# K in the outer loop of one product, and a V load placed behind two transposes, in a chunked attention and GELU kernel

## The chip, the cores and the metric

The kernel runs on one core of a Trainium2 chip. The metric is the device time of one execution in microseconds (us). The kernel before has a median of 274.94 us over three runs (272.26 to 277.09). Engines are named as the profile names them: PE is TensorE (PEld its weight loads), DVE VectorE, ACT ScalarE, POOL GpSimd, SP the engine that issues most of the transfers (SPq is its queue).

## The reference

Attention within chunks of 64 tokens, for 8 batches, 8 heads, 576 tokens and a head size of 64, and behind it a two-layer network with an exact GELU on the 4608 tokens (8 x 576) of width 512, with an inner width of 2048:

```python
scores = np.matmul(q_c, k_c.transpose(0, 1, 2, 4, 3)) / np.sqrt(D)
scores = scores - np.max(scores, axis=-1, keepdims=True)
attn = np.exp(scores)
attn = attn / (np.sum(attn, axis=-1, keepdims=True) + 1e-09)
x = np.matmul(attn, v_c)              # to (4608, 512): tokens by heads * head size
h = x @ w_in                          # (512, 2048)
g = 0.5 * h * (1.0 + erf(h / np.sqrt(2.0)))
out = g @ w_out                       # (2048, 512)
```

Inputs and output are float32; the products run in bfloat16 with float32 sums.

## The kernel before, in words

The tokens go in nine tiles of 512, numbered 0 to 8. Tiles 0 to 7 hold the first eight chunks of one batch each; tile 8 holds the ninth chunk of every batch, and its q, k and v are gathered by eight small loads each, one per batch. A tile goes through attention (which makes x, transposed, 512 by 512), mm1 (x times w_in and GELU, which makes h) and mm2 (h times w_out, which makes y). The main loop runs over t; its pass t does mm1 and mm2 of tile t and, in between the products of mm2, attention of later tiles. We call the pass "stage t".

The order of the work on every engine is the order in which the program is written: nothing reorders it later. Work that is to stand between products is handed over as lists of small functions: `e1` for mm1 (keyed by a word of a hand-written order such as `FOUR`) and `e2` for mm2 (keyed by a number from 0 to 5, called by `also(i)`).

From stage 3 on, mm2 is done with seven products of half size in place of eight (`mm2_seven`, for stages 3 to 7; stage 8 has its own, `last_seven`). h and w_out are cut into two by two blocks, and sums of blocks are multiplied. One such product has 16 matmuls of 128x128 weights by 128x256: two row blocks of 128 tokens (m), each summed over eight blocks of K (f), both halves in one PSUM bank. Its sums of h come from VectorE: s1 and s2 in pieces, at the words `h1`, `h2`, `h3` of mm1's order (blocks 0-1, 2-5 and 6-7; L549 and L550), s3 at L554 and s4 at L558. The order on TensorE in mm2 of stages 3 to 7 is:

- first product: h and w_out, into bank X, which ScalarE copies to bank Y (L752)
- at 1: attention times V of tile t + 1 (`rows_av`, L324). VectorE divides the result (L342, L344) into rows, and SP issues two transposes of these rows to x (`rows_x`, L336): one behind the second of six banks, one behind the sixth. Also at 1: casts and loads of q
- second product: s2 and T2, a difference of blocks of w_out, onto bank Y. This is the one that the change touches
- third product (onto X) and fourth (s1, onto Y)
- at 2: the scores of tile t + 2 (`quad_S`, L228), from q and k that SP transposed (`flip`, L189) during mm1
- fifth product (s3, bank Z), sixth (s4, onto Y), then at 4: four differences of blocks of x (`x_sums`, L595), which mm1 of the next stage needs from its fourth product on; then the seventh product (onto Z)

Stores of y (L815) stand behind the third, fifth, sixth and seventh products, on SP. SP also issues all loads (L102 to L141), in the order of the program. V of a tile comes in two halves (even heads, then odd heads: `load_v_rows(t, (0,))` and `(1,)`), into one arrival buffer of a pool of five; GpSimd casts both halves (L206) before `rows_av` reads them. For tile 8 the two halves are eight loads each: the first half is issued at the start of mm1 of stage 6, behind the transposes of q and k of tile 8 (`flips_of`), the second half and both casts at the start of stage 7.

Of the kernel before, what the change touches and what calls it, by code (L numbers as in the profile page):

```python
# [11 lines left out]
def kernel(  # L12
# [9 lines left out]
    nc = tc.nc  # L22
    P = 128
# [4 lines left out]
    B, H, S, D = q.shape  # L28
# [38 lines left out]
    FH, TH, NH = FF // 2, MT // 2, d_model // 2  # L67
# [17 lines left out]
    def stage_tile(pool=None):  # L85
        if pool is wsum:
            return wsum.tile([P, SW], f32, tag="wsum", name="arrival")
        return stage.tile([P, SW], f32, tag="stage", name="arrival")
# [26 lines left out]
    def load_v_rows(t, parity=range(2)):  # L115

        if "vf" not in tiles[t]:
            tiles[t]["vf"] = stage_tile()[:].rearrange("p (h n d) -> p h n d", h=H, d=D)
        raw = tiles[t]["vf"]

        def go(to, rows):
            nc.sync.dma_start(to, rows.rearrange("h key d -> key h d"))  # L122
        last = CT // 2 - 1
        if t < B and 0 in parity:
            for n in range(CT // 2):
                go(raw[:, 0::2, n], v[t, 0::2, P * n:P * (n + 1), :])
        if t < B and 1 in parity:
            for n in range(last):
                go(raw[:, 1::2, n], v[t, 1::2, CH + P * n:CH + P * (n + 1), :])
            go(raw[0:CH, 1::2, last], v[t, 1::2, MT - CH:MT, :])  # L130
            go(raw[CH:P, 1::2, last], v[t, 1::2, 0:CH, :])
        if t == B:
            for b in range(B):
                for r in parity:
                    c, n = place(r, b)
                    go(raw[CH * c:CH * (c + 1), r::2, n], v[b, r::2, MT:S, :])
# [13 lines left out]
    def place(r, i):  # L150

        return (i % 2, i // 2) if r == 0 else ((i + 1) % 2, (i - 1) % CT // 2)
# [47 lines left out]
    def cast_v_rows(t, copy):  # L200
        st = tiles[t]
        st["v"] = ld.tile([P, H, CT // 2, D + 1], bf16, tag="v", name="v_nat")
        if t >= FIRSTX:
            nc.gpsimd.memset(st["v"][:, :, :, D:], 1.0)
        for r in range(2):
            copy(st["v"][:, r::2, :, :D], st["vf"][:, r::2])  # L206
# [511 lines left out]
    def product(out, lhs, rhs, fresh, behind=lambda m: None):  # L718

        for m in range(TH // P):  # L720
            for f in range(FH):
                nc.tensor.matmul(out[m], lhs[:, f, m * P:(m + 1) * P], rhs[:, f, :],  # L722
                                 start=fresh and f == 0 and (m == 0 or len(out) == 3), stop=(f == FH - 1),
                                 skip_group_check=True)
            behind(m)

    def halves(bank):
        return [bank[:, 0], bank[:, 1]]

    def mm2_seven(t, at={}):  # L730

        def also(i):
            for u in at.get(i, ()):
                u()
        st = tiles[t]
        h = st["h"][:].rearrange("p (k f) (m e) -> p k f m e", k=2, m=2)
        w = w_out_sb[:].rearrange("p (k f) (n e) -> p k f n e", k=2, n=2)
        s = [None] + [st["s", i][:] for i in range(1, 5)]
        T = [None] + [w_t[i] for i in range(1, 5)]
        def bank_mm():  # L740
            return ps_mm.tile([P, 2, NH], f32, tag="mm", name="y_ps")
        X, Y = bank_mm(), bank_mm()
        s2, s5 = (work.tile([P, 2, NH], f32, tag=nm, name=nm, bufs=1) for nm in ("y_2", "y_5"))
        y = [ypool.tile([P, 2, d_model], f32, tag="y", name="y_sb") for _ in range(2)]
        TT, add = nc.vector.tensor_tensor, mybir.AluOpType.add
        if t == B:
            s1 = work.tile([P, 2, NH], f32, tag="y_1", name="y_1", bufs=1)
            last_seven(t, h, w, s, T, (X, Y, bank_mm()), (s1, s2, s5), y)
            return
        also(0)  # L750
        product(halves(X), h[:, 0, :, 0], w[:, 0, :, 0], True)
        AC(Y[:], X[:])  # L752
        Z = bank_mm()
        st["Z"] = Z[:].rearrange("p m n -> p (m n)")
        also(1)
        h_third(t)
        product(halves(Y), s[2], T[2], False)
        AC(s2[:], Y[:])
        product(halves(X), h[:, 1, :, 0], w[:, 1, :, 0], False)
        AC(y[0][:, :, :NH], X[:])  # L760
        store(t, 0, 0, y)
        product(halves(Y), s[1], T[1], False)
        AC(s5[:], Y[:])
        h_fourth(t)
        also(2)
        product(halves(Z), s[3], T[3], True)
        TT(y[1][:, :, NH:], Z[:], s5[:], op=add)
        store(t, 1, 1, y)
        also(3)
        product(halves(Y), s[4], w[:, 1, :, 1], False)  # L770
        AC(y[0][:, :, NH:], Y[:])
        store(t, 0, 1, y)
        also(4)
        product(halves(Z), h[:, 1, :, 1], T[4], False)
        TT(y[1][:, :, :NH], Z[:], s2[:], op=add)
        store(t, 1, 0, y)
        also(5)
# [144 lines left out]
    with tc.manual_schedule():  # L922
# [7 lines left out]
        T = att_units(0, DV, AC)  # L930
# [74 lines left out]
        T = att_units(1, AC, AC)  # L1005
# [15 lines left out]
        def flips_of(n):  # L1021
            for nm in "qk":
                flip(n, nm)
# [22 lines left out]
        for t in range(1, NT):  # L1046
            e1, e2 = {}, {}
            n = t + 1
            if n < NT:
                tiles[n]["x"] = xpool.tile([P, G, MT], bf16, tag="x", name="x")  # L1050
            if t == 1:
                flips_of(2)
                load_v_rows(2, (1,))
                cast_v_rows(2, PO)
                loads_of_qk(3)
                pool_cast_qk(3)
                e1 = {"1a": [lambda: w_in_sums(slice(0, 2), "c")], "p": [lambda: load_v_rows(3)], "end": [lambda: w_sums((1, 3))]}
                e2 = one_tile(2, {5: [lambda: act_table(Act.Gelu)],
                                  8: [lambda: flips_of(3), lambda: loads_of_qk(4)]})
            elif t == 2:  # L1060
                cast_v_rows(3, PO)
                pool_cast_qk(4)
                e1 = {f"i{g}": [lambda g=g: in_order(3, g)] for g in range(G)}
                e1.update({f"w{i}": [lambda i=i: w_sums((i,))] for i in (2, 4)})
                flips_of(4)
                load_v_rows(4)
                load_qk(5, "q")
                cast_v_rows(4, PO)
                e2 = one_tile(3, {8: [lambda: load_qk(5, "k")], 14: [lambda: quad_S(4)]})
            elif n < NT:  # L1070
                def ahead(t=t):
                    if FIRST7 < t < B - 2:
                        load_v_rows(t + 2)
                    if t + 2 < NT:
                        flips_of(t + 2)
                    if t == FIRST7:
                        load_ahead(t, "q")
                    if t == B - 2:
                        load_v_rows(B, (0,))
                    if t == B - 1:  # L1080
                        load_v_rows(B, (1,))
                        cast_v_rows(B, PO)

                def late_v(t=t):
                    load_v_rows(t + 2)
                    cast_v_rows(t + 2, PO)

                def behind(t=t):
                    load_ahead(t, "k")
                e1 = {"begin": [ahead]}  # L1090
                if t + 2 < NT:
                    e1["begin"] = [lambda t=t: pool_cast_k(t + 2), ahead]
                if t == FIRST7:
                    pool_cast_q(t + 2)
                    e1["tab"] = [lambda: act_table(Act.Gelu)]
                e2 = {1: [lambda: rows_av(n, tiles[n - 1]["Z"]), lambda: rows_x(n)], 2: [], 3: [], 4: [behind, lambda: x_sums(n)]}
                if t == FIRST7:
                    e2[2] += [late_v, lambda: w_in_sums(slice(0, 2), "d")]
                if FIRST7 < t < B - 2:
                    e2[1] += [lambda t=t: cast_v_rows(t + 2, PO)]  # L1100
                if t + 3 < NT:
                    if t > FIRST7:
                        e2[1] += [lambda t=t: load_ahead(t, "q")]
                    e2[1] += [lambda t=t: pool_cast_q(t + 3)]
                if n + 1 < NT:
                    e2[1] = [lambda: act_table(Act.Exp)] + e2[1]
                    e2[2] += [lambda: quad_S(n + 1), lambda: act_table(Act.Gelu)]
            phase(t, e1, e2, between=last_rows if t == 1 else {})
# [28 lines left out]
```

## Time and profile before

| | us |
|---|---|
| Median of three runs | 274.94 |
| The profiled execution's own time | 274.2 |
| Its span, first to last instruction | 272.5 |
| TensorE busy in the span | 259.7 (95%) |
| VectorE busy | 197.1 (72%) |
| ScalarE busy | 185.8 (68%) |
| GpSimd busy | 79.7 (29%) |
| Mean granted TensorE clock | 0.998 |

A row of a timeline gives the start, the length (both us), the engine, the line of the kernel, the operation, what it writes and reads, how many instructions are merged in the row, and in brackets how long the engine stood idle before it and what ended that wait. A group's row gives the count, then the busy time and the mean length of one in ns. Matmuls overlap in the pipeline, so the length of a row of matmuls ends some 0.16 us after the next row starts; the distance of starts is the pace.

### The profile page before, as it was taken

The page shows a single profiled execution, that of the slowest core. Times are in us where ns is not written, and L with a number is a line of the kernel's source. Part 1 is how long each engine was busy: PE and PEld are TensorE (multiplying, and loading weights), DVE is VectorE, ACT ScalarE, POOL GpSimd, SP SyncE. Part 2 cuts the span into 40 slices and gives each one's busy share as a digit, 9 for nine tenths or more (in the row PEclk, how much of TensorE's full clock was granted, in tenths as well). Part 3 has the DMA queues.
Part 4 walks back from the last instruction along what each step waited for, and adds up shares of the span by engine and source line. Part 5 has one row for each costly group of instructions (what it writes and reads, how often), then busy time and mean ns, then how long its engine had stood idle before and what let it go on. Part 6 is the DMA issues. An engine that isn't in the chain of part 4 may idle for free.

```text
span 272.5 us, 7517 instructions
## 1 busy us (share of the span) xinstructions
PE 259.7 (95%) x3057; PEld 191.5 (70%) x3057; DVE 197.1 (72%) x359; ACT 185.8 (68%) x361; POOL 79.7 (29%) x125
## 2 busy tenths in 40 slices
PE   7689999999999999999999999999999899999993
PEld 2464454486458645778888788888887788888782
DVE  2673577977895999389859956994799279946851
ACT  3567746788668965985699579956995689338600
POOL 2734667352630633330434203600340101000000
PEclk9999999999999999999999999999999999999999
DMA  6999999998979968799979999969976841440005
GB/s 194 272 364 405 395 395 241 264 278 220 327 204 265 261 149 205 221 198 270 206 193 262 211 254 262 233 132 143 238 182 127 190 128 26 77 157 2 1 2 154
DMA packets 128627, 56.60 MB, mean 208 GB/s; under 512 B 104016, under 2 KB 123472, under 8 KB 128592
## 3 DMA queue, kind: packets, MB, share of 16 engines
q1 hardware_dynamic: 128272, 55.59, 80.9%
q8 instruction: 24, 0.39, 0.5%
q10 hardware_dynamic: 320, 0.52, 0.5%
q14 instruction: 11, 0.09, 0.1%
HBM read 36.70 MB, written 9.44 MB: 169 GB/s over the span
## 4 chain that ended last, share of the span: by engine, by line
PE 79%; DVE 7%; DMA 4%; SPq 4%; ACT 2%; issue 1%; POOL 0%; DVEq 0%; ACTq 0%
PE y_ps L722 24%; PE h_Y L655 13%; PE h_Z L655 9%; PE h_X L655 8%; PE y_ps L824 7%; PE h_ps L518 5%; PE h_ps L675 4%; PE y_ps L848 4%; SPq L122 2%; DMA arrival<-in_k_dram 2%; PE s_ps L228 1%; DMA x<-x_r 1%; DVE h_s L550 1%; DVE h_s L549 1%; PE h_ps L530 1%
## 5 line engine op out<-in xcount | busy, mean ns | idle before, releaser
L655 PEld LDWEIGHTS <-w_in_s 128*128 128x128 bf16 x448 | 43.6, 97 | 8.3 <-DVE x_t L595 1.4
L722 PEld LDWEIGHTS <-h_s 128*128 128x128 bf16 x384 | 36.8, 98 | 6.1 <-DVE h_s L550 1.6
L655 PEld LDWEIGHTS <-w_in_sb 128*128 128x128 bf16 x336 | 32.7, 97 | 7.1 <-issue 1.1
L156 POOL CAST q_nat<-arrival 128x512 bf16<-128x512 f32 x33 | 20.1, 645 | 59.2 <-DMA arrival<-in_q_dram 38.2
L722 PE MATMUL y_ps<-w_t,h_s 128*128 128x256 bf16 x288 | 34.9, 273 | 0.6 <-DVE h_s L550 0.5
L824 PE MATMUL y_ps<-w_out_sb,h 128*128 128x512 bf16 x144 | 33.0, 380 | 0.3 <-ACT y_sb L835 0.3
L655 PE MATMUL h_Y<-x_t,w_in_s 128*128 128x256 bf16 x224 | 31.4, 272 | 1.3 <-DVE x_t L595 1.1
L156 POOL CAST k_nat<-arrival 128x512 bf16<-128x512 f32 x34 | 24.0, 742 | 29.1 <-DMA arrival<-in_k_dram 26.2
L655 PE MATMUL h_X<-x,w_in_sb 128*128 128x256 bf16 x224 | 31.6, 273 | 0.0
L722 PEld LDWEIGHTS <-h 128*128 128x128 bf16 x288 | 28.1, 98 | 3.8
L206 POOL CAST v_nat<-arrival 128x1024 bf16<-128x1024 f32 x14 | 15.4, 1100 | 47.6 <-DMA arrival<-in_v_dram 47.2
L824 PEld LDWEIGHTS <-h 128*128 128x128 bf16 x144 | 13.4, 97 | 15.7 <-issue 0.8
L688 ACT COPY h_Y<-h_X 128x512 f32<-128x512 f32 x28 | 15.8, 581 | 10.9 <-PE h_X L655 10.7
L722 PE MATMUL y_ps<-w_out_sb,h 128*128 128x256 bf16 x192 | 22.9, 273 | 0.0
L920 ACT ACT_TABLE_LOAD x16 | 20.5, 1283 | 1.0 <-PEq L1121 0.7
L701 DVE COPY h_a<-h_Y 128x512 f32<-128x512 f32 x8 | 5.5, 692 | 18.4 <-PE h_Y L655 18.4
L662 ACT ACTIVATE h<-h_X 128x512 bf16<-128x512 f32 x28 | 16.6, 598 | 1.6 <-PE h_X L655 1.0
L662 ACT ACTIVATE h<-h_Y 128x512 bf16<-128x512 f32 x28 | 16.5, 595 | 1.5 <-PE h_Y L655 1.1
L655 PE MATMUL h_Z<-x_t,w_in_s 128*128 128x256 bf16 x112 | 16.8, 273 | 0.0
L655 PE MATMUL h_Z<-x_t,w_in_sb 128*128 128x256 bf16 x112 | 16.5, 272 | 0.3 <-DVE h_b L704 0.3
L655 PE MATMUL h_Y<-x,w_in_s 128*128 128x256 bf16 x112 | 16.4, 273 | 0.0
L235 ACT ACTIVATE pT<-s_ps 128x512 bf16<-128x512 f32 x28 | 14.4, 607 | 1.5 <-PE s_ps L228 1.5
(143 smaller groups left out, 473.3 us busy)
## 6 DMA issues: line engine op xcount, KB each, us to landing
out_dram<-y_sb SPq DMA_DIRECT2D x32, 256.0 KB, 3.6
arrival<-in_q_dram SPq DMA_DIRECT2D x7, 1024.0 KB, 6.3
arrival<-in_k_dram SPq DMA_DIRECT2D x24, 256.0 KB, 5.7
arrival<-in_v_dram SPq DMA_DIRECT2D x42, 128.0 KB, 3.2
arrival<-in_moe_w_out_dram SPq DMA_DIRECT2D x4, 1024.0 KB, 12.0
arrival<-in_v_dram SPq DMA_DIRECT2D x8, 256.0 KB, 6.1
arrival<-in_moe_w_in_dram SPq DMA_DIRECT2D x4, 512.0 KB, 6.8
arrival<-in_moe_w_in_dram SPq DMA_DIRECT2D x2, 1024.0 KB, 10.1
```

What stands on the lines that cost most here:

```text
L156: copy(st[nm][:, g].rearrange("p j r d -> p r j d"), st[nm + "f"][:, 2 * g:2 * g + 2])
L206: copy(st["v"][:, r::2, :, :D], st["vf"][:, r::2])
L235: nc.scalar.activation(pT[:].rearrange("p u (c j) -> p u c j", j=J), s_ps[g2][c][:].rearrange("p u (j c) -> p u c j", j=J), Act.Exp, scale ...
L518: nc.tensor.matmul(h_ps[a][:], w_in_sb[:, ks, f * P:(f + 1) * P], st["x"][:, ks, :], start=(ks == 0), stop=(ks == KS - 1))
L655: nc.tensor.matmul(banks[g + name][:, i], lhs[:, kk, i], rhs[:, kk], start=fresh and i == kk == 0, stop=(kk == 1), skip_group_check=True)
L662: nc.scalar.activation(h[:, j:j + 2, m], src[:], Act.Gelu)
L675: nc.tensor.matmul(bank[:], w_in_sb[:, ks, f * P:(f + 1) * P], st["x"][:, ks, :], start=(ks == 0), stop=(ks == KS - 1))
L688: AC(banks[g + "Y"][:], banks[g + "X"][:])
L722: nc.tensor.matmul(out[m], lhs[:, f, m * P:(m + 1) * P], rhs[:, f, :], start=fresh and f == 0 and (m == 0 or len(out) == 3), stop=(f == FH ...
L824: nc.tensor.matmul(y_ps[:], st["h"][:, f, ms * P:(ms + 1) * P], w_out_sb[:, f, :], start=(f == 0), stop=(f == FF - 1))
L848: nc.tensor.matmul(tiles[t]["y_ps", ms][:], tiles[t]["h"][:, f, ms * P:(ms + 1) * P], w_out_sb[:, f, :], start=(f == 0), stop=False)
L920: nc.scalar.activation(act_scratch[:], rest[:, 0:1], func)
```

## The change

The second product of `mm2_seven` is written with the loop over f (K) outside and the loop over m inside, by a function of its own; `halves(Y)` are the two halves of bank Y. The first half of V of tile 8 is no longer issued at the start of mm1 of stage 6 but in mm2 of stage 6, at 1, behind `rows_av` and `rows_x` (B is 8, so t == B - 2 is stage 6).

```diff
+    def product_by_f(out, lhs, rhs):
+
+        for f in range(FH):
+            for m in range(TH // P):
+                nc.tensor.matmul(out[m], lhs[:, f, m * P:(m + 1) * P], rhs[:, f, :], start=False, stop=(f == FH - 1),
+                                 skip_group_check=True)
+
...
         also(1)
         h_third(t)
-        product(halves(Y), s[2], T[2], False)
+        product_by_f(halves(Y), s[2], T[2])
         AC(s2[:], Y[:])
...
                     if t == FIRST7:
                         load_ahead(t, "q")
-                    if t == B - 2:
-                        load_v_rows(B, (0,))
                     if t == B - 1:
                         load_v_rows(B, (1,))
                         cast_v_rows(B, PO)
...
                 if FIRST7 < t < B - 2:
                     e2[1] += [lambda t=t: cast_v_rows(t + 2, PO)]
+                if t == B - 2:
+                    e2[1] += [lambda: load_v_rows(B, (0,))]
```

## The prediction

> **What bounds the kernel now.** I read four views: the chain of waits, the table of windows for TensorE cut at the first matmul of each half stage, the timelines of single engines around those cuts, and the rows of single tiles for the landing of transfers. "Stage t" is the pass of the main loop for token tile t; each has a first product (mm1, into h) and a second (mm2, into y).
>
> The page's span, and its chain by engine:
>
> ```profile
> span 272.5 us, 7517 instructions
> PE 79%; DVE 7%; DMA 4%; SPq 4%; ACT 2%; issue 1%; POOL 0%; DVEq 0%; ACTq 0%
> ```
>
> TensorE carries the chain, so only gaps in TensorE are worth anything. The windows (length, then busy time and count, granted clock, DMA share, GB/s) are: mm2 of stage 3, mm1 and mm2 of stage 4, mm2 of 5, mm1 and mm2 of 6, mm1 and mm2 of 7:
>
> ```profile
> 121.60:135.48 13.88, 13.86 (x242) 1.00 1.06 221
> 135.48:147.84 12.36, 12.36 (x115) 1.00 0.94 226
> 147.84:162.19 14.35, 14.15 (x242) 1.00 1.05 221
> ...
> 174.56:188.63 14.07, 14.02 (x242) 1.00 0.88 159
> 188.63:201.35 12.72, 12.47 (x115) 1.00 1.03 212
> 201.35:215.70 14.35, 14.03 (x243) 1.00 0.71 132
> 215.70:229.38 13.68, 12.54 (x115) 1.00 0.47 128
> 229.38:242.48 13.10, 13.08 (x179) 1.00 0.34 82
> ```
>
> The same work has an undisturbed length: 12.36 for mm1 (stage 4), 13.88 for mm2 (stage 3). What exceeds it is what there is to win: mm2 of stages 4, 5, 6 lose 0.47, 0.19 and 0.47; mm1 of stage 6 loses 0.36 and mm1 of stage 7 loses 1.32. Stage 7's mm2 has no scores to compute and is shorter for that.
>
> **The second product with K outside.** In stage 4 (rows of TensorE, its weight loads, VectorE and the SP queue, and the landing of the transpose of k):
>
> ```profile
> 150.46 0.94 PE L722 MATMUL y_ps<-w_t,h_s 128*128 128x256 bf16 x6
> 150.79 0.33 PEld L722 LDWEIGHTS <-h_s 128*128 128x128 bf16 x4 [0.23 <-DVE h_s L550]
> 151.58 0.99 PEld L722 LDWEIGHTS <-h_s 128*128 128x128 bf16 x10 [0.46 <-DVE h_s L550]
> 156.27 0.62 PEld L228 LDWEIGHTS <-k_t 64*64 64x64 bf16 x64 [0.21 <-DMA k_t<-k_nat]
> ...
> 149.33 1.41 DVE L550 TENSOR_TENSOR h_s<-h_s,h 128x1024 bf16<-128x1024 bf16 x1
> 151.10 0.42 DVE L550 TENSOR_TENSOR h_s<-h_s,h 128x512 bf16<-128x512 bf16 x1
> ...
> 151.96 1.94 SPq L189 DMA_TRANSPOSE k_t<-k_nat  x1
> ...
> DMA to landing us min/median/max: 4.2/4.2/4.2
> ```
>
> The product reads h_s in eight blocks of K; VectorE makes them in three pieces (blocks 0-1, 2-5, 6-7), the last two by the two L550 rows, ending at 150.74 and 151.52. With m outside, block 2 is the third matmul and block 6 the seventh, hence two stops. With K outside they are the fifth and the thirteenth. The pace is 1.31/12 = 0.109 us a matmul:
>
> ```profile
> 162.36 1.31 PE h_X L655 x12
> ```
>
> Block 2 is then wanted at 150.46 + 4 x 0.109 = 150.90 and block 6 at 150.46 + 12 x 0.109 = 151.77, both after their pieces. The stop goes wholly, in each of the three stages that have one; stages 3 and 7 have none and get nothing.
>
> What is late next decides how much stays. Stage 4: the scores (L228) started at 156.27, and that row names the transpose of k, which landed at 151.96 + 4.2 = 156.16. It hangs on casts and on the SP queue ahead of it, not on this product. A wake-up costs 0.06 (block 6's piece ended at 151.52, the load came at 151.58), so the scores can't start before 156.22: of 0.47 only 0.05 stays. Bounds: 0 and 0.47.
>
> Stages 5 and 6: the fifth product (Z) needs the third h sum, L554, which stands on VectorE behind the rows of x, a chain that begins when the last piece of h_s is done and which this change doesn't move.
>
> ```profile
> 181.78 1.22 DVE L554 TENSOR_TENSOR h_s<-h 128x2048 bf16<-128x2048 bf16 x1
> 183.38 0.83 PE L722 MATMUL y_ps<-w_t,h_s 128*128 128x256 bf16 x6
> ...
> 208.84 1.22 DVE L554 TENSOR_TENSOR h_s<-h 128x2048 bf16<-128x2048 bf16 x1
> 210.45 1.92 PE L722 MATMUL y_ps<-w_t,h_s 128*128 128x256 bf16 x16
> ```
>
> In stage 5 L554 ends at 183.00, so Z could start at 183.06, 0.32 earlier than it did: its 0.19 passes whole. In stage 6 it ends at 210.06, Z can't start before 210.12, 0.33 earlier: of 0.47, 0.33 stays. The sum of this part is 0.05 + 0.19 + 0.33 = 0.57, between 0 and 1.13.
>
> The number of matmuls and weight loads stays; what is new is that the output goes to the other half of the bank at each matmul, and that K is outermost. The nearest rows are mm1's above, which changes halves every second matmul at 0.109, and stage 0's second product, which has K outside over four banks:
>
> ```profile
> 34.23 0.86 PE y_ps L848 x4
> ...
> L915 PE MATMUL warm<-rest 128*128 128x512 bf16 x13 | 5.1, 516 | 1.2 <-DVE rest L47 1.2
> L848 PE MATMUL y_ps<-w_out_sb,h 128*128 128x512 bf16 x48 | 11.9, 379 | 0.3 <-ACT h L521 0.3
> ```
>
> 0.86/4 = 0.215 us for 512 columns is 0.1075 for 256, no slower. So I take zero; the far end, a matmul slowed as the first ones of the kernel are (516 against 379 ns, 0.069 for 256 columns), is a rival below.
>
> The Trainium skill, "TensorE: Matmul & The Clock Gate", section "Loop structure matters more than you think", speaks against this order: it wants all K tiles of one output tile in a row, because a loop with K outside that waits for data at each step lets the clock fall to half. Its condition, a long wait in each step, is not met in these rows: the windows show a granted clock of 1.00 in every half stage, with gaps of at most about one microsecond.
>
> **The V load behind the transposes.** Around the end of stage 6 (SP queue, VectorE, TensorE, the landing of all transposes of x):
>
> ```profile
> 204.33 2.10 SPq L189 DMA_TRANSPOSE k_t<-k_nat  x1
> 206.48 5.25 SPq L122 DMA_DIRECT2D arrival<-in_v_dram  x8
> 211.84 3.20 SPq L336 DMA_TRANSPOSE x<-x_r  x2
> 215.13 4.59 SPq L815 DMA_DIRECT2D out_dram<-y_sb  x4
> 219.77 5.24 SPq L122 DMA_DIRECT2D arrival<-in_v_dram  x8
> ...
> 205.95 0.62 DVE L344 TENSOR_TENSOR x_r<-av_ps,one 128x448 bf16<-128x448 f32 x1
> 208.63 0.29 DVE L344 TENSOR_TENSOR x_r<-y_ps,one 128x128 bf16<-128x128 f32 x1
> 212.46 0.69 DVE L767 TENSOR_TENSOR y_sb<-y_ps,y 128x512 f32<-128x512 f32 x1 [1.27 <-ACT pT L235]
> 217.16 0.76 DVE L595 TENSOR_TENSOR x_t<-x 128x512 bf16<-128x512 bf16 x2 [4.01 <-DMA x<-x_r]
> ...
> 215.70 1.47 PE L655 MATMUL h_X<-x,w_in_sb 128*128 128x256 bf16 x12
> 218.31 0.61 PE L655 MATMUL h_Y<-x_t,w_in_s 128*128 128x256 bf16 x4 [1.14 <-DVE x_t L595]
> ...
> DMA to landing us min/median/max: 2.9/3.4/6.4
> ```
>
> The rows of x were ready at 206.57 (first seven blocks) and 208.92 (rest), but eight V loads held the SP queue until 211.73. So x came late, VectorE waited 4.01 us for it, and TensorE, done with three products from x itself, stood until 218.31. The change puts the V loads after both transposes.
>
> Then the first transpose goes at 206.57 (k's has left the queue at 206.43) and the second at 208.92; with the median 3.4 it lands at 212.3, with the slowest, 6.4, at 215.3. VectorE is free after L767, at 213.15, and needs 1.15 to the sum that TensorE stood for (217.16 to 218.31): ready at 214.3, at worst 216.5. TensorE wants it at 215.70 + 1.31 = 217.0, some 0.6 earlier with the first part's gain, 216.4. So the wait goes and mm1 of stage 7 falls to 12.36: 1.32 gained. Less only if 0.36 is lost there as in stage 6, whose cause I don't know: bounds 0.96 and 1.32.
>
> What the loads were moved in front of: nothing but the four stores of stage 6. The second transpose takes up to 1.6 (half of 3.20), to 210.5; eight loads of 5.25, to 215.8; the stores start 0.6 later than their 215.13. Behind them stand the other eight V loads, so at worst 0.6 later than 219.77. Who waits for those:
>
> ```profile
> 227.01 1.05 POOL L206 CAST v_nat<-arrival 128x1024 bf16<-128x1024 f32 x1 [11.50 <-DMA arrival<-in_v_dram]
> 231.22 0.66 PE L324 MATMUL av_ps<-v_nat,pT 64*64 64x65 bf16 x57
> ```
>
> The cast would end at 227.01 + 0.6 + 1.05 = 228.7; TensorE reads it at 231.22 - 1.9 = 229.3. The first half's cast is ahead of that one. Covered, with 0.6 us left in the worst count; should that cover fail, a cost of the same size as the delay.
>
> **The sum.** 0.57 + 1.32 = 1.89. The profiled execution took 274.2 (span 272.5 and 1.7 around it), so 272.3 by its own measure; the median of the three runs is 274.94, from which it would be 273.05. I put down 272.6, between the two.
>
> **The rivals.** First, only the V part pays: the stops in mm2 all move to the transpose of k or to L554. For it: stage 4's row; against it: 0.32 of room in stage 5. Gain 1.3, 272.9 on the profile's measure, 273.6 on the median's. Chance 0.15.
>
> Second, more than I count: the transpose of k lands sooner and VectorE's chain moves up, so that all 1.13 stays and stage 6's 0.36 goes too: 1.32 + 1.13 + 0.36 = 2.8, 271.4. Against it: nothing in the change touches what is ahead of k's transpose in stage 4. Chance 0.07.
>
> Third, x stays late for another reason, for instance a transpose slowed beyond the slowest seen: only 0.57 stays, 273.6 to 274.4. For it: the first transpose now follows k's directly. Chance 0.07.
>
> Fourth, slower: the new order itself costs TensorE time, at each of the 5 x 16 = 80 matmuls in the five products. It turns the gain into a loss from 1.89/80 = 0.024 us a matmul; at the far end of the rows, 0.069, it is 5.5 us, and the time 274.2 - 1.9 + 5.5 = 277.8. Against it stand the paces of 0.109 and 0.1075. Chance 0.04. By the rule of the Trainium skill named above, a clock at half, it would be 80 x 0.109 = 8.7 us and 281.0; the clock column gives that no support.
>
> Fifth, the edit does not do what it says: the order on the queues of the built program shows the eight V loads after the two transposes, and the waits at the fifth and thirteenth matmul, so hardly. The forecast has the rest, 0.67.
>
> **How the numbers follow.** The terms alone span 271.4 to 274.4. The runs of one kernel lie between 272.26 and 277.09, so a median can sit a microsecond or more off; I take the range from 270.2 (272.26 less 1.9, rounded down a little) to 275.2 (277.09 less 1.9). The fourth rival lies outside. Two per cent, 5.5 us, is about what this kernel's measurement can tell from no change: three runs lie 4.8 apart. No case gains that much, so faster by over 2% has 0.05, for what I haven't seen; slower by over 2% needs the worst of the fourth, 0.03; within 2%, 0.92.
>
> **What would show it.** The second product has no stop by L550 in stages 4 to 6; the scores of stage 4 still start on k's transpose; Z in stage 6 starts right behind L554; on SP both transposes of x follow k's and the V loads end near 216; mm1 of stage 7 is 12.4 long without a wait for x_t; the last V cast ends before rows_av. The prediction is wrong if matmuls of the new loop pace above 0.13, if stage 7's mm1 keeps 13 or more, or if V is what TensorE waits for at the end of stage 7's first product.

## The result, and the profile after

The changed kernel takes 272.81 us in the median of 21 runs, the kernel before 274.83 us in 21. The ratio is 0.9948, with a 95% interval of 0.9923 to 0.9973: a gain of 1.4 us, between 0.7 and 2.1. Forecast were 272.6 and a gain of 1.89. Ratios, here and below, compare the fast runs alone and medians cover all runs, so a ratio is not quite the quotient of two medians. The profiled execution has a span of 271.5 us, 1.0 less than before.

The windows for TensorE, cut as in the prediction (length, then busy time and count, clock, DMA share, GB/s): mm2 of stage 4, mm2 of 5, mm1 and mm2 of 6, mm1 of 7. From L727 on, line numbers are 7 higher than before, and the new product is L731.

```profile
148.96:162.83 13.87, 13.85 (x243) 1.00 1.13 204
...
175.19:189.27 14.08, 13.92 (x242) 1.00 1.09 169
189.27:201.98 12.71, 12.46 (x114) 1.00 0.99 204
201.98:215.97 13.99, 13.97 (x243) 1.00 0.66 135
215.97:228.33 12.36, 12.36 (x114) 1.00 0.55 149
```

Against before (14.35, 14.07, 12.72, 14.35, 13.68): mm2 of stage 4 lost 0.48, stage 5 nothing, mm2 of 6 lost 0.36, mm1 of 7 lost 1.32. From the start of mm2 of stage 3 to the end of mm2 of stage 7 it is 241.43 - 122.65 = 118.78 us, against 242.48 - 121.60 = 120.88: 2.10 less. But this execution came to that point 1.05 later. The chain of waits says why:

```profile
11.90 7.17 DMA arrival<-in_moe_w_in_dram
19.13 0.63 POOL w_in_sb L903
```

It waited for w_in at the start, some 100 us before anything that the change touches (the first changed product is in stage 3). That is the scatter of one execution, and it is nearly as large as the effect.

The end of stage 6 (SP queue, VectorE, TensorE) is the part that answers to the rows shown of before:

```profile
205.39 1.63 SPq L189 DMA_TRANSPOSE k_t<-k_nat  x1
207.25 3.58 SPq L336 DMA_TRANSPOSE x<-x_r  x2
210.88 6.12 SPq L122 DMA_DIRECT2D arrival<-in_v_dram  x8
217.10 2.25 SPq L822 DMA_DIRECT2D out_dram<-y_sb  x4
...
213.34 0.75 DVE L595 TENSOR_TENSOR x_t<-x 128x512 bf16<-128x512 bf16 x2
...
215.97 1.47 PE L655 MATMUL h_X<-x,w_in_sb 128*128 128x256 bf16 x12
217.28 0.60 PE L655 MATMUL h_Y<-x_t,w_in_s 128*128 128x256 bf16 x4
```

Both transposes go ahead of the V loads, the differences of x are made at 213.34 with no wait in brackets (before: 217.16, after a wait of 4.01), and h_Y follows h_X at once.

The last piece of the sums, the third sum and the fifth product in the same stage 6:

```profile
204.93 0.72 DVE L550 TENSOR_TENSOR h_s<-h_s,h 128x512 bf16<-128x512 bf16 x1
...
209.45 1.22 DVE L554 TENSOR_TENSOR h_s<-h 128x2048 bf16<-128x2048 bf16 x1
...
210.72 1.92 PE L722 MATMUL y_ps<-w_t,h_s 128*128 128x256 bf16 x16
```

The piece ends 3.67 us after the start of mm2 (205.65 - 201.98), as late as before (3.68), but the fifth product starts 8.74 after it and not 9.10, 0.05 behind the end of L554.

### The profile page after: what moved, and what is told of

Read it like the earlier page. It is cut to its first block, busy times and chain, and to the rows that moved or that the text cites. A ratio compares the mean times of both kernels' runs of the same rounds, so it can differ in the third digit from the quotient of the medians.

```text
span 271.5 us, 7517 instructions
## 1 busy us (share of the span) xinstructions
PE 259.1 (95%) x3057; PEld 192.1 (71%) x3057; DVE 197.0 (73%) x359; ACT 186.0 (69%) x361; POOL 81.8 (30%) x125
## 4 chain that ended last, share of the span: by engine, by line
PE 76%; SPq 8%; DMA 7%; DVE 3%; ACT 2%; issue 1%; POOL 0%; DVEq 0%; ACTq 0%
PE y_ps L722 22%; PE h_Y L655 12%; PE h_Z L655 8%; PE h_X L655 8%; PE y_ps L831 7%; PE h_ps L518 5%; SPq L122 4%; PE h_ps L675 4%; PE y_ps L855 4%; PE y_ps L731 3%; DMA arrival<-in_moe_w_in_dram 3%; DMA k_t<-k_nat 2%; SPq L141 2%; DMA arrival<-in_v_dram 2%; PE s_ps L228 2%
## 5 line engine op out<-in xcount | busy, mean ns | idle before, releaser
L156 POOL CAST q_nat<-arrival 128x512 bf16<-128x512 f32 x33 | 21.4, 689 | 58.1 <-DMA arrival<-in_q_dram 28.4
L722 PEld LDWEIGHTS <-h_s 128*128 128x128 bf16 x304 | 29.4, 98 | 3.6
L206 POOL CAST v_nat<-arrival 128x1024 bf16<-128x1024 f32 x14 | 16.2, 1154 | 47.8 <-DMA arrival<-in_v_dram 47.8
L722 PE MATMUL y_ps<-w_t,h_s 128*128 128x256 bf16 x208 | 24.7, 273 | 0.0
L701 DVE COPY h_a<-h_Y 128x512 f32<-128x512 f32 x8 | 5.5, 691 | 19.4 <-PE h_Y L655 19.4
```

Source lines behind the costliest of these rows:

```text
L156: copy(st[nm][:, g].rearrange("p j r d -> p r j d"), st[nm + "f"][:, 2 * g:2 * g + 2])
```

## The experiments

Lengths in us of the half stages that matter, from the first matmul to the first matmul of the next (undisturbed: mm2 13.88, mm1 12.36):

| execution | mm2 of 4 | mm2 of 5 | mm1 of 6 | mm2 of 6 | mm1 of 7 |
|---|---|---|---|---|---|
| before | 14.35 | 14.07 | 12.72 | 14.35 | 13.68 |
| before, second profile | 14.40 | 14.16 | 12.71 | 15.12 | 13.68 |
| product alone | 13.87 | 14.46 | 12.71 | 14.74 | 13.81 |
| V move alone | 13.96 | 13.96 | 12.71 | 13.96 | 12.36 |
| V move alone, again | 13.87 | 14.11 | 12.71 | 13.87 | 12.36 |
| changed | 13.87 | 14.08 | 12.71 | 13.99 | 12.36 |
| changed, again | 14.70 | 14.81 | 12.71 | 13.91 | 12.36 |
| K outside in all products | 13.88 | 14.25 | 12.71 | 13.90 | 12.36 |
| all V ahead (m outside) | 13.88 | 13.96 | 12.71 | 19.92 | 14.76 |

**The two parts alone.** The product alone leaves the load where it was; the V move alone takes the product back:

```diff
-        product_by_f(halves(Y), s[2], T[2])
+        product(halves(Y), s[2], T[2], False)
```

> Only the second product is changed; the V load stands where it stood before. Theory one (the new order takes away the stops by the last piece of h_s, and what stays of it depends on the transpose of k and on L554): mm2 of stages 4, 5 and 6 come to 13.9 to 14.1 us each, mm1 of stage 7 keeps its loss (13.4 to 13.9, because x comes a little later against TensorE), and the time falls by 0.3 to 0.9 us, a ratio of 0.997 to 0.999. Theory two (the stops come and go with the time at which GpSimd casts V beside the sums of h, and the order has no part in it): mm2 of stages 4 to 6 lies anywhere from 13.9 to 14.4, as before, and the ratio is 1.000.

> Only the load of the first half of the ninth V is moved; all products have m outside. Theory one (the V loads held up the SP queue ahead of the transposes of x): mm1 of stage 7 is 12.36 us long with no wait for x_t, the time falls by about 1.3 us, a ratio of 0.995; mm2 of stages 4 to 6 keeps stops by L550 of up to 0.47 in those stages in which a cast of V runs beside the sums of h. Rival (the wait for x would come from something else): mm1 of stage 7 keeps 13 us or more, ratio 1.000.

The product alone: 275.59 us in the median of 12 runs, ratio 1.0031 (0.9997 to 1.0066). The V move alone: 273.23 of 12, ratio 0.9966 (0.993 to 1.0002). The V move does at mm1 of stage 7 what was forecast. The product alone gains nothing, and mm2 of stage 6 and mm1 of stage 7 show where its gain would go: together they are 2.3 us over their undisturbed length. There is no stop in the second product of stage 6; instead TensorE waits 0.56 for x at the start of mm1 of stage 7, and again for x_t. The eight V loads held the SP queue for 6.29 us in this execution (5.25 in the first of before), and with them in front x lands when the queue lets it, whenever TensorE comes.

The surprise is the V move alone: with m outside, the stops should have been there, and mm2 is 0.08 over its undisturbed length in each of the three stages. The sums of h in its stage 4 (VectorE), and GpSimd beside them:

```profile
151.80 0.68 DVE L549 TENSOR_TENSOR h_s<-h 128x1024 bf16<-128x1024 bf16 x1
152.51 1.41 DVE L550 TENSOR_TENSOR h_s<-h_s,h 128x1024 bf16<-128x1024 bf16 x1
...
152.05 1.33 POOL L206 CAST v_nat<-arrival 128x1024 bf16<-128x1024 f32 x1 [1.47 <-DMA arrival<-in_v_dram]
```

And in stage 4 of the kernel before, then of the changed kernel:

```profile
148.21 1.08 DVE L549 TENSOR_TENSOR h_s<-h 128x1024 bf16<-128x1024 bf16 x1
...
149.12 1.07 POOL L206 CAST v_nat<-arrival 128x1024 bf16<-128x1024 f32 x1 [0.19 <-DMA arrival<-in_v_dram]
```

```profile
150.04 0.69 DVE L550 TENSOR_TENSOR h_s<-h_s,h 128x1024 bf16<-128x1024 bf16 x1
151.11 0.42 DVE L550 TENSOR_TENSOR h_s<-h_s,h 128x512 bf16<-128x512 bf16 x1
...
151.58 1.91 PE L731 MATMUL y_ps<-w_t,h_s 128*128 128x256 bf16 x16
```

A sum of 128 by 1024 takes 0.68 to 0.69 us alone and up to 1.53 beside a cast, in stage 5 of the kernel before:

```profile
175.65 1.53 DVE L550 TENSOR_TENSOR h_s<-h_s,h 128x1024 bf16<-128x1024 bf16 x1
...
175.59 1.05 POOL L206 CAST v_nat<-arrival 128x1024 bf16<-128x1024 f32 x1 [1.21 <-DMA arrival<-in_v_dram]
```

The sum waits for the cast to end. In all 17 cases in these traces in which such a sum started with 0.15 us or more of a cast of V still to run, it ended 0.53 to 0.55 behind that cast (here 177.18 and 176.64), however long the cast was. Where the sum started first, it kept 0.68 to 0.69 (in 12 of 13 cases) and the cast was the longer one, up to 1.56 where a cast alone takes 1.04.

What counts for the old order is when the last piece ends. The second product starts 2.62 us after the start of mm2 and wants block 6 another 6 x 0.109 = 0.65 later, at 3.27. In stage 4 the last piece ended at 3.68 with two sums stretched (before: 1.08 and, in the prediction's row, 1.41), which stops TensorE for 0.47; at 3.29 with one stretched (V move alone), for 0.08; and at 2.60 in the second profile of the V move alone, for nothing. In stage 6 the casts beside the sums are those of k. When a cast runs is set by the landing of V or k, which differs from one execution to the next. In the changed kernel's stage 4 the last piece was ready at 151.53, before the product began at 151.58: there the old order would not have stopped either. The Trainium skill, "GPSIMD Engine Reference", section "8. Key points", says that GpSimd shares its interfaces to SBUF with VectorE and names VectorE's instructions with two SBUF inputs, which L549 and L550 are; these rows agree, and show that the later of the two waits for the earlier.

**The suspected costs doubled.** All V ahead puts the other eight loads in front of the transposes too; K outside in all products makes 30 more products in the new order.

```diff
                     if t == B - 2:
-                        load_v_rows(B, (0,))
+                        load_v_rows(B, (0, 1))
                     if t == B - 1:
-                        load_v_rows(B, (1,))
```

```diff
     def product(out, lhs, rhs, fresh, behind=lambda m: None):

+        if len(out) == 2:
+            for f in range(FH):
+                for m in range(TH // P):
+                    nc.tensor.matmul(out[m], lhs[:, f, m * P:(m + 1) * P], rhs[:, f, :],
+                                     start=fresh and f == 0 and m == 0, stop=(f == FH - 1), skip_group_check=True)
+            return
```

> The kernel before, with the second eight loads of the ninth V put ahead of the transposes too, behind the first eight: the suspected cost doubled. If the SP queue holds the transposes, both go 5.2 to 6 us later than before, x_t as well, and mm1 of stage 7 grows by that much, from 13.7 to about 19, so the time grows by about 5 us (ratio about 1.02). If the wait of before was set elsewhere, mm1 of stage 7 stays near 13.7 and the ratio near 1.00.

> The changed kernel, with K in the outer loop of all seven products of stages 3 to 7 (30 more products, 480 more matmuls in the new order). If the order costs TensorE nothing, each product keeps a pace of 0.109 us a matmul and the time is that of the changed kernel within 0.3 us (ratio to the kernel before 0.994 to 0.997). If the order cost 0.024 us a matmul, the time would be 480 x 0.024 = 11.5 us above the changed kernel's (ratio about 1.037).

All V ahead took 281.65 us in its one run, against a median of 274.43 for the kernel before: 7.2 more, where about 5 were expected. The SP queue and TensorE at the end of its stage 6:

```profile
206.74 11.54 SPq L122 DMA_DIRECT2D arrival<-in_v_dram  x16
218.40 2.69 SPq L336 DMA_TRANSPOSE x<-x_r  x2
...
221.73 2.74 PE L655 MATMUL h_X<-x,w_in_sb 128*128 128x256 bf16 x12 [5.76 <-DMA x<-x_r]
```

The first transpose goes 218.40 - 211.84 = 6.6 us later than before (6.1, counted from the start of mm2 of stage 6), and TensorE now waits 5.76 us for x itself. So the SP queue holds the transposes, as forecast; but the wait falls at the end of mm2 of stage 6 (19.92), and mm1 of stage 7 is 14.76 and not about 19. Most of what mm1 of stage 7 has over its undisturbed length is TensorE's clock after that wait, told below.

K outside in all products: 272.76 us in the median of 8, ratio 0.9939 (0.9904 to 0.9974), the changed kernel's time. Mm2 of stages 4 and 6 is 13.88 and 13.90. A cost of 0.024 us at each of 480 matmuls would be 11.5 us; there is none. Two of its stages are longer for other reasons: in stage 5 (14.25) the scores waited for the transpose of k, and mm2 of stage 7 is 13.56 long in place of 13.10. There the cast of the second half of V began at 227.74, just ahead of a sum of h at 227.99, which took 1.33; L554 came late by that, and the fifth product waited for it.

**The kernel before, once more**, for a second profile:

> The kernel before, unchanged, for a second profile. If the stops by L550 depend on whether a cast of V runs beside the sums of h, they need not come back at the same size: mm2 of stages 4, 5 and 6 lies anywhere between 13.9 and 14.4 us, and goes with the lengths of L549 and L550 in that stage (both long: near 14.35; one long: near 13.96; none: 13.88). If they are a fixed cost of the order, stages 4 and 6 show 14.35 again. Mm1 of stage 7 keeps its loss, 13.4 to 13.9, by both.

```profile
151.50:165.90 14.40, 14.03 (x242) 1.00 1.07 221
178.27:192.43 14.16, 14.01 (x242) 1.00 1.11 176
205.14:220.26 15.12, 14.09 (x243) 1.00 0.65 121
220.26:233.94 13.68, 12.54 (x112) 1.00 0.46 128
...
210.15 6.70 SPq L122 DMA_DIRECT2D arrival<-in_v_dram  x8
216.96 2.65 SPq L336 DMA_TRANSPOSE x<-x_r  x2
...
220.26 1.48 PE L655 MATMUL h_X<-x,w_in_sb 128*128 128x256 bf16 x12 [1.01 <-DMA x<-x_r]
```

The stop in stage 4 came back, the one in stage 6 did not: mm2 of 6 has 1.24 over its undisturbed length, but 1.01 of it is TensorE waiting for x, since the same eight loads took 6.70 us of the queue, not 5.25. With mm1 of 7 the V loads cost some 2.3 us in this execution, 1.32 in the first. Its single time, 278.85 us, is long mostly for a reason that lies elsewhere, at the start of the kernel, below.

**Loads moved in the other stages.** Three kernels put the nine V loads of stages 4 and 5, which stand ahead of the transposes of q and k, elsewhere: behind these (so directly ahead of the transposes of x), or behind the transposes of x, once with each order of the product.

```diff
-                    if FIRST7 < t < B - 2:
-                        load_v_rows(t + 2)
                     if t + 2 < NT:
                         flips_of(t + 2)
+                    if FIRST7 < t < B - 2:
+                        load_v_rows(t + 2)
```

```diff
-                    if FIRST7 < t < B - 2:
-                        load_v_rows(t + 2)
...
                 if FIRST7 < t < B - 2:
-                    e2[1] += [lambda t=t: cast_v_rows(t + 2, PO)]
+                    e2[1] += [lambda t=t: load_v_rows(t + 2), lambda t=t: cast_v_rows(t + 2, PO)]
```

> The changed kernel, with the nine V loads of stages 4 and 5 put behind the transposes of q and k and so directly ahead of the transposes of x, as the moved loads stood in stage 6 of the kernel before. If loads ahead of the transposes of x are what costs, x comes 3 to 5 us later at the end of stages 4 and 5, mm1 of stages 5 and 6 (or the end of mm2 before them) grows by 1 to 3 us each, and the time is 2 to 5 us above the changed kernel's (ratio to the kernel before 1.002 to 1.013). If the case of stage 6 was special, nothing changes but that k's transpose lands sooner, and the ratio stays at 0.994 to 0.996.

> The changed kernel, with the nine V loads of stages 4 and 5 put behind the transposes of x as well, as the change did for stage 6. The transposes of q and k then go about 5 us sooner in stages 4 and 5, and the casts of V no longer fall beside the sums of h. Mm2 of stages 4 and 5 comes to 13.88 us, with no wait for the transpose of k; against it stands that the loads of q and k behind V start later, so that the casts and transposes of the next stage could be late. If that cover holds, the time is 0 to 0.4 us below the changed kernel's (ratio to the kernel before 0.993 to 0.995); if it fails, stage 5 or 6 grows by 1 us or more.

> The run with all V loads behind the transposes of x, with m in the outer loop of the second product again. If the stops by L550 come from casts of V beside the sums of h, there are none in stages 4 and 5 now (13.88 to 13.96 each) and the new order is worth nothing there: the same time as with K outside, within 0.2 us. If they come from the order alone, mm2 of stages 4 to 6 shows 14.1 to 14.35 and the time is 0.5 to 1.1 us longer.

Ahead of the transposes of x: 275.49 us of 10, ratio 1.0045 (1.0004 to 1.0085), some 2.7 us above the changed kernel, within the expected 2 to 5, but only in part for the expected reason. Up to the end of mm2 of stage 5 nothing is lost (13.87, 12.36, 13.87): at the end of stage 4 there was room for a later x. At the end of stage 5 there was not: VectorE waited 3.16 us for x, and TensorE's first product from x_t in mm1 of stage 6 started at 191.07, 0.47 later than 189.29 + 1.31. The rest of that mm1, 14.43 long, went in small waits for VectorE, whose copy h_sb (L701) itself waited 1.19. The last part is mm2 of stage 7, 13.55 long, with the cast of V beside a sum as in the run with K outside in all products.

Behind the transposes of x: 280.93 us of 6, ratio 1.0239 (1.019 to 1.0288), against an expected 0.993 to 0.995. Mm1 of stage 5 grew to 14.08 and mm1 of stage 6 to 17.51. The SP queue, VectorE and TensorE around stage 6:

```profile
187.58 5.88 SPq L122 DMA_DIRECT2D arrival<-in_v_dram  x9
193.51 3.91 SPq L111 DMA_DIRECT2D arrival<-in_q_dram  x8
197.86 1.82 SPq L822 DMA_DIRECT2D out_dram<-y_sb  x3
...
205.56 0.69 DVE L701 COPY h_sb<-h_Y 128x512 f32<-128x512 f32 x1 [4.51 <-DMA out_dram<-y_sb]
...
206.31 0.97 PE L655 MATMUL h_Y<-x,w_in_s 128*128 128x256 bf16 x4 [3.38 <-DVE h_sb L701]
```

The V loads and the q loads behind them pushed the stores of y back to 197.86; VectorE's copy h_sb takes a buffer of the pool from which y is stored, and waited 4.51 us for a store to land. This is the cover that the prediction named for the stores: in stage 6 no q or k load stands behind V, so it holds there, and in stages 4 and 5 it doesn't.

With m outside it is the same (281.9 us of 6, ratio 1.0252, 1.0195 to 1.0308), and mm2 of stage 4 is 13.87 by both orders, as expected where no cast falls beside a sum for long. Stage 5 missed the expected 13.88 to 13.96: it is 14.45 with m outside and 14.21 with K outside, since casts of k now fell beside its sums (0.90 and 0.98 with m outside). Stage 6 is 14.23 and 14.22. In both the stop by L550 is there with m outside and gone with K outside, and with K outside the fifth product waits for L554 instead. The late loads brought other waits besides, so these are no clean measure of the order.

**The sums made late.** To see what the order can give at most, the last piece of the sums is made twice in stages 4 to 7:

```diff
                 if t >= FIRST7:
                     h_sums(t, *hs[word])
+                if word == "h3" and four:
+                    h_sums(t, *hs[word])
```

> The V load moved, m in the outer loop, and in stages 4 to 7 the last piece of the h sums (L549 and L550 for blocks 6 and 7) is made twice, so that it ends 0.84 us later. Block 6 is then the seventh matmul of the second product and stops it: by either theory mm2 of stages 4 to 6 grows by about 0.8 to 0.9 us, from about 13.96 to 14.7 to 14.9 each.

> The changed kernel with the same doubled piece, so K is outside and block 6 is the thirteenth matmul, 0.65 us later. If VectorE's chain from the last piece of h_s through the rows of x to L554 caps what the order can give, the fifth product waits for L554 and mm2 of stages 4 to 6 comes out only about 0.3 us below the run with m outside, 14.4 to 14.6 each. If nothing caps it, the whole 0.65 us shows, 14.1 to 14.2 each.

The lengths missed: 15.04, 15.35 and 15.14 with m outside, 15.65, 15.25 and 15.11 with K outside, because casts fell beside the sums, and in stage 4 with K outside the scores waited for the transpose of k. What tells the theories apart is the distance from the last piece to the fifth product. Stage 5, VectorE and TensorE, with m outside, then with K outside:

```profile
181.12 0.42 DVE L550 TENSOR_TENSOR h_s<-h_s,h 128x512 bf16<-128x512 bf16 x1
...
186.96 1.92 PE L724 MATMUL y_ps<-w_t,h_s 128*128 128x256 bf16 x16
```

```profile
180.33 0.42 DVE L550 TENSOR_TENSOR h_s<-h_s,h 128x512 bf16<-128x512 bf16 x1
184.57 1.22 DVE L554 TENSOR_TENSOR h_s<-h 128x2048 bf16<-128x2048 bf16 x1
...
185.84 1.92 PE L724 MATMUL y_ps<-w_t,h_s 128*128 128x256 bf16 x16 [0.25 <-DVE h_s L554]
```

From 181.54 to 186.96 it is 5.42 us, from 180.75 to 185.84 it is 5.09; stage 6 has the same two numbers. With K outside the fifth product starts 0.05 behind the end of L554 and names it. So the cap is there: the order gives at most 5.42 - 5.09 = 0.33 us a stage, not 0.65. The 5.42 also holds where nothing was doubled (in stages 4 and 6 of the kernel before the piece ends at 3.68 and the fifth product starts at 9.10, counted from the start of mm2), so it tells below what m outside would have cost in an execution with K outside.

**Both once more on one chip.**

> The changed kernel, timed beside the V move alone on one chip. By the stage lengths seen so far (V move alone 13.96 in mm2 of stages 4 to 6, changed kernel 13.87 to 14.08) the two are within 0.4 us of each other, ratio to the kernel before 0.993 to 0.996 for both. If the order of the second product is worth the 0.57 us that was predicted, this one is 0.002 lower in ratio than the V move alone.

> The V move alone again, beside the changed kernel: 0.993 to 0.997 by the reading that the V move carries the gain; 0.998 or more if the product carries most of it.

The changed kernel: 272.92 us of 12, ratio 0.995 (0.9914 to 0.9986). The V move alone: 273.31 of 12, ratio 0.9954 (0.9915 to 0.9993). In this profile of the changed kernel the weight loads of the scores in stages 4 and 5 read:

```profile
155.98 0.62 PEld L228 LDWEIGHTS <-k_t 64*64 64x64 bf16 x64 [1.04 <-DMA k_t<-k_nat]
183.15 0.62 PEld L228 LDWEIGHTS <-k_t 64*64 64x64 bf16 x64 [1.15 <-DMA k_t<-k_nat]
```

Both stages waited for the transpose of k (mm2 of 14.70 and 14.81). A TensorE that comes there sooner by the new order only waits longer.

## Why the prediction was right, and where not

- **The total** was right: 1.89 forecast, 1.4 measured (0.7 to 2.1). The V part carries it, as forecast; the part of the product was sized too large. That the profiled execution shows even more (2.10 between the same two points) is partly luck: the 0.48 that its mm2 of stage 4 lost is not the order's, as no cast fell beside the sums there in that execution.
- **The V load behind the transposes**: shown. In all ten profiled executions with the move, mm1 of stage 7 is 12.36 or 12.37; in the four without it, 13.68 to 14.76. Doubling the loads in front made a wait of 5.76 us. The term, 1.32, is what the first profile gave; the second gave 2.3, as the loads took 6.70 us and x itself was late. Timed alone the move gave ratios of 0.9966 and 0.9954, so 0.9 and 1.3 us, each give or take about 1. On the chip where both parts were timed alone, the medians are 273.23 for the move and 275.59 for the product.
- **The cover of the stores and the second V half**: it held in the changed kernel, whose second-half cast ended at 227.84 with its reader at 230.17 and mm2 of stage 7 at 13.10 as before. The stores started at 217.10, later than the "0.6 at worst" behind 215.13, since the eight loads took 6.12 us and not 5.25; nobody waited for them. What the prediction did not ask is what else the cast touches: TensorE reaches stage 7 sooner, the cast need not, and in two of the ten executions (K outside in all products, and the loads ahead of the transposes of x) it fell beside a sum of h and mm2 of stage 7 lost 0.46 and 0.45. That the cover of the stores is not general was shown by V behind the transposes in stages 4 and 5.
- **The second product**: this step failed in its size, 0.57. It took the stops of one execution for a property of the order. The runs show that they go with the casts that run beside the sums of h, between 0 and 0.52 a stage. What did the order give, then? An estimate from the rows of each execution: with m outside the fifth product starts 5.42 behind the last piece, and not before 8.62. Against that, K outside saved 0.35 in the changed kernel (all in stage 6; in stage 5 the transpose of k held the scores, and the fifth product started at 8.83, before at 8.82, with the piece at 3.40 in both), nothing in its second profile, and 0.52 with K outside in all products (0.09, 0.10 and 0.33 in stages 4, 5 and 6). The timings can't resolve so little: without the V move the product gains nothing (1.0031, 0.9997 to 1.0066), and beside it the ratio is lower by 0.0004 on one chip and, with K outside in all products, by 0.0027 on another, with intervals of about 0.004 each way.
- **The caps**: the one by L554 was right, 0.33 measured against 0.32 and 0.33, and in stage 6 of the changed kernel the fifth product starts right behind L554, as said. The one by the transpose of k was right as a mechanism (it is in the changed kernel's stage 5, and in stages 4 and 5 of its second profile) but not as a number of a stage: it moves from one execution to the next. In the changed kernel's stage 4, where the prediction put it, the scores started without it.
- **The rivals**: "only the V part pays", given 0.15, is nearer to what the runs show than the forecast was. "The order costs TensorE time" fell: 480 more such matmuls, same time. "X stays late for another reason" fell too: no execution with the move shows a wait for x at the start of mm1 of stage 7. The rule of the Trainium skill on the order of loops ("TensorE: Matmul & The Clock Gate", section "Loop structure matters more than you think") rests on a wait for data at each step; here the blocks are in SBUF and the windows show a clock of 1.00.

## What to carry to other kernels

A stop seen once is not a term of a sum: look at what set its size (here a cast on another engine, timed by a transfer), and whether it would come again. In a queue that works in the order of the program, a transfer that nobody waits for yet belongs behind the one that somebody waits for, but ask each time what then stands behind it; the same move that helped at the end of the kernel left it 2.4% slower than before when made in the two stages ahead of that, because it held back stores and so a buffer. And a saving ahead of a wait that another queue has set is not a saving until that wait is gone.

## What the runs showed of the hardware

TensorE's clock fell after long gaps and took microseconds to return. In the run with all V ahead, two-microsecond windows after the gap of 5.76 us, which ended at 221.73, read:

```profile
218.00:220.00 2.00, 0.00 (x0) 0.95 0.55 120
220.00:222.00 2.00, 0.27 (x2) 0.50 0.98 186
222.00:224.00 2.00, 2.00 (x11) 0.50 1.06 316
224.00:226.00 2.00, 2.00 (x11) 0.50 0.36 119
226.00:228.00 2.00, 2.00 (x18) 0.84 0.39 131
228.00:230.00 2.00, 2.00 (x21) 1.00 0.00 0
```

Half the clock for about five microseconds of matmuls, which is most of what mm1 of stage 7 had over 12.36 there (14.76). After the gap of 3.38 us in the run with V behind in stages 4 and 5 too, the windows read 0.60 and 0.55 for four microseconds (four matmuls in 0.97 against 0.60), while gaps of up to 1.3 us left it at 1.00. The Trainium skill, "TensorE: Matmul & The Clock Gate", section "Why this matters for your kernels", asks for no gaps above about 3 us; these rows agree.

The clock near the start of the kernel is not the same in each execution: the window from 8 to 12 us reads 1.00 in the first profile of the kernel before and 0.50 in the second.

```profile
8.00:12.00 4.00, 3.33 (x71) 1.00 1.13 291
```

```profile
8.00:12.00 4.00, 3.71 (x51) 0.50 0.89 214
```

In the second it stays at 0.50 up to 20 us, and the 16 matmuls of L465 that take 1.09 us in the first take 1.90 there. Mm1 of stage 3 starts at 108.32 us in the first and at 111.99 in the second, two executions of one program: more than the whole effect studied here. How much of the 3.67 is the clock's and how much comes from loads is not separated by these runs.
